# The last layer of a stacked cross network: tail sums by GpSimd, four row tiles in column tiles, another order of row tiles and stores

## The chip, the cores and the metric

The kernel runs on one core of one Trainium2 chip. Its time is the device time of one execution in microseconds (us); the median of several executions is given. A profile is one more execution, recorded by the hardware profiler; its span reaches from the first to the last recorded event of the program, and is shorter than the execution's own time.

The engines are TensorE (PE; the loads of its stationary operand are shown as PEld), VectorE (DVE), ScalarE (ACT), GpSimd (POOL) and SyncE (SP). Matmuls write PSUM, which has eight banks of 128 partitions by 512 float32; GpSimd does not read PSUM in this kernel.

## The reference

Six layers of a cross network over 4096 rows of 416 features (26 fields of 16), all in bfloat16:

```python
B, F, D, L = 4096, 26, 16, 6
Din = min(F * D, 1024)              # 416
x0: (B, Din)   ws: (L, Din, Din)   bs: (L, Din)

def reference(x0, ws, bs):
    x = x0
    for l in range(ws.shape[0]):
        x = x0 * (x @ ws[l] + bs[l]) + x
    return x
```

Since every layer adds a multiple of x0, x after layer l is x0 * (1 + the sum of all x @ w + b so far). The kernel keeps that sum, in PSUM.

## The kernel before

**Tiling.** The rows are worked in four blocks of 1024 (NS, SB), each block through all six layers before the next. The 416 features are three chunks of 128 (`CH`) and a tail of 32. Inside a block the data lies transposed: features on partitions, rows along the free dimension, in two halves of 512 rows. Six PSUM banks hold the running sums of the main chunks, bank 3h + m for half h and chunk m; banks 6 and 7 hold those of the tail, four groups of 256 rows stacked on 32 partitions each. Bank contents stay over the layers: each layer's matmuls add to them.

**One layer.** `main` (288) multiplies one chunk pair in four column tiles: four matmuls, each with 32 columns of weights, write one strip of 32 partitions each, at tile position (0, 32q). `tail_rows` (302) adds the tail features' share, in row tiles: 32 partitions of the contraction at position (32q, 0), with all 128 columns. `tail_outs` (344) makes the tail's own sums, in column tiles. A switch between column tiles, row tiles and the whole array happens several times in a layer. `leave` (404) then makes the next x of a chunk on DVE: (sum + bias) * x0. `leave_tail` (426) does it for the tail: ACT adds the bias in two halves (`tail_halves`, 417; one half for each of banks 6 and 7) and writes the float32 tile `t32`, and GpSimd multiplies it by x0. `cb` holds 1 plus the running sums of the biases, one column for each layer; its chunk NC is the tail's.

**The last layer of the last block.** The first three blocks leave their results transposed and turn them by DMA. The last block's last layer is computed in row form instead, so that no turn is needed: eight tiles of 128 rows by 416 features, one PSUM bank each, `ROW_BANKS` (580): tile 0 has bank 6, tile 1 bank 7, tiles 2 to 7 banks 0 to 5. Each tile is a sum of three parts:

- `row_main` (584): x of layer 5 (128 features by 128 rows, stationary) times the weights (416 wide, moving), three matmuls.
- `row_sums` (594): the running sums up to layer 4, which lie transposed in `sS` as bfloat16, are turned by a product with the identity matrix, three matmuls with 128 moving columns.
- `row_tails` (604): the tail's share of the product and the tail's running sums `st`, four row groups at once, for tiles 0, 2, 4, 6 and then for tiles 1, 3, 5, 7. The matmul that opens a bank carries a start flag.

`keep_sum` (440) makes `sS` from the main banks, plus the last layer's bias, and `tail_halves(L - 1, st_sb, ...)` (565) makes `st` from the tail banks. These run in the branch `ending` (529, 564 to 574): ACT does the two halves of `st`, the three sums of the first half of rows and one of the second; DVE does the other two. A bank can be overwritten by a row tile when its sums are read out.

`finish` (626) multiplies a tile by x0's rows (`xr`): DVE does six tiles straight from PSUM; tiles 1 and 3 are copied by ACT to float32 and multiplied by GpSimd. `store_rows` (645) stores finished tiles, 104 KB each.

**What sets the order.** Each engine runs its instructions in the order in which the program adds them (`Plan.add`, 28); a table of readers and writers puts in the semaphore waits. A reader of a PSUM bank also waits for the earlier readers of that bank. A DMA waits on the queue of the engine that issues it, and what stands behind it on that queue waits too. The order of the last layer is written out by hand at 652 to 673: PE does mains 0 to 3, sums 0 to 3, main 4, the row tails, sums 4, and then main and sums of tiles 5, 6, 7. Tiles 1 and 3 stand on ACT ahead of ACT's stores. The stores are SP: tiles 0 and 1; ACT: 2 and 3; SP: 4 and 5; ACT: 6; SP: 7. At last SP waits for all landings.

Of the kernel before, what the change touches and what calls it, by code (L numbers as in the profile page):

```python
# [6 lines left out]
FP32 = mybir.dt.float32  # L7
ALU = mybir.AluOpType
# [110 lines left out]
def bass_standalone__dcn_v2_cross__recsys_kernel(  # L119
# [7 lines left out]
    L = ws.shape[0]  # L127
    NC = 3
# [13 lines left out]
    with ExitStack() as es:  # L142

        def sb(name, shape, dt=BF16):
            return es.enter_context(nc.sbuf_tensor(name, shape, dt))
# [22 lines left out]
        bsa_sb = sb("bsa_sb", [L + 1, D])  # L168
        u_sb = sb("u_sb", [L + 1, L])
        cb_sb = sb("cb_sb", [128, NC + 1, L], FP32)  # L170
        ps = es.enter_context(nc.psum_tensor("ps", [128, 8, 512], FP32))
        psT = ps.bitcast(BF16)

# [4 lines left out]
        def quad(q):  # L178
            return slice(32 * q, 32 * q + 32)
# [78 lines left out]
        def mm(pe, dst, lhsT, rhs, start, pos=None):  # L258
            return pe.matmul(  # L259
                dst, lhsT=lhsT, rhs=rhs, start=start, stop=True, skip_group_check=True,  # L260
                tile_position=pos,
            )
# [154 lines left out]
        def tail_halves(l, dst, key):  # L417
            for h in HALVES:
                p = slice(64 * h, 64 * h + 64)
                P.add(  # L420
                    "scalar", lambda e, p=p, h=h: e.activation(  # L421
                        out=dst[p, :], in_=ps[p, T_BANK[h], 0:G], func=ACTF.Identity, bias=cb_sb[p, NC, l:l + 1]
                    ), reads=[("ps", T_BANK[h]), ("cb",)], parts=[key],
                )
# [15 lines left out]
        def keep_sum(h, c, eng):  # L440
            o, i, b = sS_sb[:, c, h * H:(h + 1) * H], ps[:, bank(h, c), :], cb_sb[:, c, L - 1:L]
            if eng == "scalar":
                fn = lambda e: e.activation(out=o, in_=i, func=ACTF.Identity, bias=b)
            else:
                fn = lambda e: e.tensor_scalar_add(o, i, b)
            P.add(eng, fn, reads=[("ps", bank(h, c)), ("cb",)], writes=[("sS", c, h)])
# [80 lines left out]
        for s in range(NS):  # L527
            for l in range(L):
                ending = s == NS - 1 and l == L - 2
                if s == NS - 1 and l == L - 1:  # L530
                    break
                if s == 0 and l == 0:
                    for k in CH:
                        for m in CH:
                            main(s, l, 0, m, k)
                        if k == 0:
                            bias_sums()
                        if k == 1:
                            tail_in(0)
                    tail_outs(s, l, True)  # L540
                    tail_rows(s, l, False)
                    for c in CH:
                        leave(s, l, 0, c)
                else:
                    for m in CH:
                        for k in CH:
                            main(s, l, 0, m, k)
                    tail_rows(s, l, l == 0)
                    for c in CH:
                        leave(s, l, 0, c)  # L550
                    tail_outs(s, l, False)
                if l == 2 and s < NS - 1:
                    tail_in(s + 1)
                leave_tail(s, l, not ending)
                if l == 2 and s < NS - 1:
                    keep_tail_in(s + 1)
                if s == 0 and l == 0:
                    corner(2, L, "wt2")
                if l == 1 and s > 0:
                    store_block(s - 1)  # L560
                if s < NS - 1 and l in (3, 4):
                    g = 2 * (l - 3)
                    swap(x0t_sb[:, s + 1], ("x0t", s + 1), tuple("scalar" if q // 2 == l - 3 else None for q in range(4)))
                if ending:
                    tail_halves(L - 1, st_sb, ("st",))
                    for c in CH:
                        keep_sum(0, c, "scalar")
                for m in CH:
                    for k in CH:
                        main(s, l, 1, m, k)  # L570
                    leave(s, l, 1, m)
                if ending:
                    for c in CH:
                        keep_sum(1, c, ("scalar", "vector", "vector")[c])
            if s < NS - 1:
                transpose_block(s)

# [3 lines left out]
        src, off = src_main(s, l)  # L581
        srct, tkey = src_tail(s, l)

        def row_main(j, start):
            b, h = ROW_BANKS[j], j // 4
            for k in CH:
                P.add(
                    "tensor", lambda pe, k=k: mm(
                        pe, ps[:, b, 0:D], src[:, k, off + j * 128:off + (j + 1) * 128], w_sb[:, l, k, :],
                        start and k == 0,  # L590
                    ), reads=[("w", l), src_key(s, l, k, h)], adds=[("ps", b)],
                )

        def row_sums(j):
            b, h = ROW_BANKS[j], j // 4

            def fn(pe):
                for c in CH:
                    ins = mm(pe, ps[:, b, c * 128:(c + 1) * 128], sS_sb[:, c, j * 128:(j + 1) * 128], ident[:, :], False)
                return ins  # L600

            P.add("tensor", fn, reads=[("ident",)] + [("sS", c, h) for c in CH], adds=[("ps", b)])

        def row_tails():
            for r in range(2):
                def fn(pe, r=r):
                    for g in range(4):
                        b = ROW_BANKS[2 * g + r]
                        mm(
                            pe, ps[:, b, 0:D], srct[quad(g), 0, r * 128:(r + 1) * 128], wt_sb[quad(g), l, :],  # L610
                            2 * g + r > 4, (32 * g, 0),
                        )
                    for g in range(4):
                        b = ROW_BANKS[2 * g + r]
                        ins = mm(
                            pe, ps[:, b, DF:D], st_sb[quad(g), r * 128:(r + 1) * 128], ident[quad(g), quad(g)],
                            False, (32 * g, 0),
                        )
                    return ins

                P.add(
                    "tensor", fn, reads=[("wt", wkey(l)), tkey, ("st",), ("ident",)],
                    adds=[("ps", ROW_BANKS[2 * g + r]) for g in range(4)],
                )

        def finish(j, by_pool):
            b, jj = ROW_BANKS[j], (NS - 1) * JS + j
            if by_pool is None:
                P.add(
                    "vector", lambda e: e.tensor_tensor(  # L630
                        out=o_sb[:, jj, :], in0=ps[:, b, 0:D], in1=xr_sb[:, j, :], op=ALU.mult
                    ), reads=[("ps", b), ("xr",)], writes=[("ol", j)],
                )
                return
            t = f32_sb[:, by_pool, :]
            P.add(
                "scalar", lambda e: e.activation(out=t, in_=ps[:, b, 0:D], func=ACTF.Copy),  # L637
                reads=[("ps", b)], writes=[("f32", by_pool)],
            )
            P.add(  # L640
                "gpsimd", lambda e: e.tensor_tensor(out=o_sb[:, jj, :], in0=t, in1=xr_sb[:, j, :], op=ALU.mult),  # L641
                reads=[("f32", by_pool), ("xr",)], writes=[("ol", j)],
            )

        def store_rows(queue, a, b):
            ja = (NS - 1) * JS
            P.add(
                queue, lambda e: e.dma_start(out_v[:, ja + a:ja + b, :], o_sb[:, ja + a:ja + b, :]),
                reads=[("ol", j) for j in range(a, b)], writes=[("outl", a)], dma="outl%d" % a,
            )  # L650

        for j in range(4):
            row_main(j, True)
        for j in range(4):
            row_sums(j)
        row_main(4, True)
        row_tails()
        finish(0, None)
        finish(1, 0)
        finish(2, None)  # L660
        finish(3, 1)
        row_sums(4)
        finish(4, None)
        for j in range(5, 8):
            row_main(j, False)
            row_sums(j)
            finish(j, None)
        store_rows("sync", 0, 2)
        store_rows("scalar", 2, 4)
        store_rows("sync", 4, 6)  # L670
        store_rows("scalar", 6, 7)
        store_rows("sync", 7, 8)
        P.add("sync", None, reads=[("out", s) for s in range(NS - 1)] + [("outl", a) for a in (0, 2, 4, 6, 7)])

        P.emit(nc, es)

# [27 lines left out]
```

## Time and profile before

| | us |
|---|---|
| median of 3 runs | 130.01 (129.94, 130.01, 130.77) |
| the profiled execution, its own time | 130.68 |
| its span | 129.4 |
| PE busy (matmuls) | 124.5, 96% of the span |
| DVE, ACT, POOL busy | 98.9, 50.5, 38.7 |
| first matmul of the row tiles starts | 119.69 |
| row tails start on PE | 123.10 |
| last matmuls of tile 7 start (three) | 125.70 |
| first product of `finish` on DVE | 123.54 |
| last product of `finish` on DVE, start and duration | 126.07, 0.59 |
| stores issued by SP | 125.39, 125.81, 126.69 |
| stores issued by ACT | 126.33, 126.79 |
| from issue to landing, stores of `o_sb` at 648 (least, median, most) | 2.1, 2.4, 2.6 |

Times in the timeline count from the span's start. A line of the timeline has start, duration, engine, line of the kernel, operation, output <- inputs, shapes and how many instructions were merged; for a matmul, 128*32 is a stationary operand of 128 rows by 32 columns (a column tile), 32*128 a row tile, 128*128 the whole array. What stands in brackets is the engine's idle time before the line and who ended it. SPq and ACTq are those engines' queues, where the duration is that of issuing, not of the transfer. TensorE's granted clock was 1.00 throughout.

### The profile page before, as it was taken

The page shows a single profiled execution, that of the slowest core. Times are in us where ns is not written, and L with a number is a line of the kernel's source. Part 1 is how long each engine was busy: PE and PEld are TensorE (multiplying, and loading weights), DVE is VectorE, ACT ScalarE, POOL GpSimd, SP SyncE. Part 2 cuts the span into 40 slices and gives each one's busy share as a digit, 9 for nine tenths or more (in the row PEclk, how much of TensorE's full clock was granted, in tenths as well). Part 3 has the DMA queues.
Part 4 walks back from the last instruction along what each step waited for, and adds up shares of the span by engine and source line. Part 5 has one row for each costly group of instructions (what it writes and reads, how often), then busy time and mean ns, then how long its engine had stood idle before and what let it go on. Part 6 is the DMA issues. An engine that isn't in the chain of part 4 may idle for free.

```text
span 129.4 us, 5183 instructions
## 1 busy us (share of the span) xinstructions
PE 124.5 (96%) x2352; PEld 64.3 (50%) x2352; DVE 98.9 (76%) x151; ACT 50.5 (39%) x113; POOL 38.7 (30%) x86
## 2 busy tenths in 40 slices
PE   6999999999999999999999999999999999999990
PEld 4544545545545545545545545545545545544650
DVE  0309879779779779788788788798797797797881
ACT  1525225455505224464514233463513243245720
POOL 6044344044024053043123152142122152242050
PEclk9999999999999999999999999999999999999999
DMA  3989999999729307000019208000009507000007
GB/s 111 232 206 223 145 245 213 173 195 170 221 51 156 64 11 262 5 0 5 0 39 193 42 0 268 0 5 0 5 16 132 120 5 263 5 0 5 0 0 263
DMA packets 34065, 13.11 MB, mean 101 GB/s; under 512 B 25334, under 2 KB 34044, under 8 KB 34044
## 3 DMA queue, kind: packets, MB, share of 16 engines
q1 hardware_dynamic: 33248, 12.20, 45.2%
q10 hardware_dynamic: 796, 0.59, 1.4%
q8 instruction: 18, 0.29, 1.0%
q14 instruction: 3, 0.02, 0.1%
HBM read 4.07 MB, written 3.41 MB: 58 GB/s over the span
## 4 chain that ended last, share of the span: by engine, by line
PE 92%; DVE 2%; DMA 2%; ACT 0%; issue 0%
PE ps L259 91%; DVE o_sb L630 2%; DMA xin_sb<-in_x_dram 2%; PE ps L482 1%; ACT x0t_sb L382 0%; PE ps L267 0%
## 5 line engine op out<-in xcount | busy, mean ns | idle before, releaser
L411 DVE SCALAR_TENSOR_TENSOR xT_sb<-ps,cb_sb,x0T_sb 128x512 bf16<-128x512 f32 x120 | 80.9, 743 | 19.8 <-PE ps L259 19.8
L259 PE MATMUL ps<-xT_sb,w_sb 128*32 128x512 bf16 (+1 forms) x1596 | 84.6, 364 | 0.0
L259 PEld LDWEIGHTS ps<-xT_sb,w_sb 128*32 128x32 bf16 x1596 | 40.8, 97 | 37.2 <-issue 4.0
L421 ACT ACTIVATE t_sb<-ps,cb_sb 64x256 f32<-64x256 f32 x46 | 21.6, 470 | 51.1 <-PE ps L259 50.9
L434 POOL TENSOR_TENSOR xt_sb<-t_sb,x0t_sb 128x256 bf16<-128x256 f32 x20 | 13.4, 672 | 63.8 <-ACT t_sb L421 63.8
L398 ACT ACTIVATE xt_sb<-xt_sb 32x256 bf16<-32x256 bf16 x38 | 15.7, 414 | 15.4 <-POOL xt_sb L434 15.2
L259 PE MATMUL ps<-x0T_sb,w_sb 128*32 128x512 bf16 (+1 forms) x336 | 19.5, 373 | 0.1
L400 POOL COPY xt_sb<-xt_sb 32x256 bf16<-32x256 bf16 x38 | 15.0, 394 | 2.4
L411 DVE SCALAR_TENSOR_TENSOR xo_sb<-ps,cb_sb,x0T_sb 128x512 bf16<-128x512 f32 x18 | 12.1, 743 | 2.5 <-PE ps L259 2.5
L259 PEld LDWEIGHTS ps<-x0T_sb,w_sb 128*32 128x32 bf16 x336 | 8.4, 97 | 8.1 <-issue 0.8
L259 PE MATMUL ps<-xt_sb,wt_sb 32*128 32x512 bf16 (+1 forms) x152 | 11.6, 326 | 0.0
L259 PE MATMUL ps<-xt_sb,wc_sb 32*128 32x256 bf16 x76 | 7.3, 268 | 0.0
L259 PEld LDWEIGHTS ps<-xt_sb,wt_sb 32*128 32x128 bf16 x152 | 2.3, 91 | 8.1 <-DVE xT_sb L411 6.4
L259 PE MATMUL ps<-w_sb,xT_sb 128*128 128x416 bf16 x24 | 5.0, 339 | 0.0
L434 POOL TENSOR_TENSOR xot_sb<-t_sb,x0t_sb 128x256 bf16<-128x256 f32 x3 | 2.0, 674 | 9.9 <-ACT t_sb L421 9.9
L398 ACT ACTIVATE x0t_sb<-x0t_sb 32x256 bf16<-32x256 bf16 x12 | 4.9, 410 | 0.1
L252 POOL COPY wc_sb<-wt_sb 32x32 bf16<-32x32 bf16 (+1 forms) x12 | 2.8, 234 | 5.5 <-DMA wt_sb<-in_ws_dram 4.9
L267 PE MATMUL ps<-ones_sb 128*128 128x256 bf16 x12 | 2.9, 419 | 1.3 <-DVE ones_sb L228 1.3
L259 PEld LDWEIGHTS ps<-xt_sb,wc_sb 32*128 32x128 bf16 x76 | 3.9, 93 | 0.3
L497 DVE COPY x0T_sb<-ps 128x256 bf16<-128x256 bf16 x4 | 1.2, 292 | 3.6 <-PE ps L482 3.4
L630 DVE TENSOR_TENSOR o_sb<-ps,xr_sb 128x416 bf16<-128x416 f32 x6 | 3.1, 584 | 1.0 <-PE ps L259 1.0
L641 POOL TENSOR_TENSOR o_sb<-f_sb,xr_sb 128x416 bf16<-128x416 f32 x2 | 1.9, 976 | 4.8 <-ACT f_sb L637 4.8
(40 smaller groups left out, 34.5 us busy)
## 6 DMA issues: line engine op xcount, KB each, us to landing
out_dram<-o_sb SPq DMA_DIRECT2D x3, 832.0 KB, 4.2
w_sb<-in_ws_dram SPq DMA_DIRECT2D x6, 312.0 KB, 5.0
xr_sb<-in_x_dram SPq DMA_DIRECT2D x1, 832.0 KB, 5.8
wt_sb<-in_ws_dram SPq DMA_DIRECT2D x4, 104.0 KB, 3.1
out_dram<-o_sb SPq DMA_DIRECT2D x2, 208.0 KB, 2.2
xin_sb<-in_x_dram ACTq DMA_DIRECT2D x1, 208.0 KB, 3.2
xin_sb<-in_x_dram SPq DMA_DIRECT2D x1, 208.0 KB, 2.9
out_dram<-o_sb ACTq DMA_DIRECT2D x1, 208.0 KB, 2.4
```

Of the source, the lines that this page charges most:

```text
L252: "gpsimd", lambda e, p=p, g=g: e.tensor_copy(out=wc_sb[p, a:b, g % 2, quad(g)], in_=wt_sb[p, a:b, DF:D]), reads=[("wt", name), ("wc", nam ...
L259: return pe.matmul(dst, lhsT=lhsT, rhs=rhs, start=start, stop=True, skip_group_check=True, tile_position=pos,)
L267: ins = pe.matmul(ps[:, 7, 0:256], lhsT=ones_sb[:, 0:128], rhs=ones_sb[:, :], start=True, stop=True)
L398: fn = lambda e, d=dst, s=src: e.activation(out=d, in_=s, func=ACTF.Copy)
L400: fn = lambda e, d=dst, s=src: e.tensor_copy(out=d, in_=s)
L411: "vector", lambda e: e.scalar_tensor_tensor(out=dst, in0=ps[:, bank(h, c), :], scalar=cb_sb[:, c, l:l + 1], in1=x0T_sb[:, c, o:o + H], op ...
L421: "scalar", lambda e, p=p, h=h: e.activation(out=dst[p, :], in_=ps[p, T_BANK[h], 0:G], func=ACTF.Identity, bias=cb_sb[p, NC, l:l + 1]), re ...
L434: "gpsimd", lambda e: e.tensor_tensor(out=dst, in0=t, in1=x0t_sb[:, s, 0, :], op=ALU.mult),
L482: ins = pe.transpose(out=psT[:, b, j * 128:(j + 1) * 128], in_=xin_sb[:, 2 * i + j, c * 128:(c + 1) * 128], identity=ident[:, :],)
L497: "vector", lambda e, d=dst, s=src: e.tensor_copy(out=d, in_=s),
L630: "vector", lambda e: e.tensor_tensor(out=o_sb[:, jj, :], in0=ps[:, b, 0:D], in1=xr_sb[:, j, :], op=ALU.mult), reads=[("ps", b), ("xr",)], ...
L641: "gpsimd", lambda e: e.tensor_tensor(out=o_sb[:, jj, :], in0=t, in1=xr_sb[:, j, :], op=ALU.mult),
```

## The change

In the branch `ending`, `st` is no longer made by ACT from PSUM. GpSimd makes it from `t32`, which holds the same sums plus layer 4's bias: it subtracts two columns of `cb` into a new tile `bt` of 128x1, and adds that to `t32`. Sum (1, 1) goes from DVE to ACT. The mains and sums of row tiles 0 to 3 are each cut into four column tiles of 32 rows; tiles 4 to 7 stay whole. The mains of tile 4 come behind the row tails instead of ahead of them, so that each of the tiles 4 to 7 has its sums right behind its mains; tile 4's bank is opened by the row tails. The stores are six instead of five, in another order and on other queues.

```diff
--- before.py
+++ after.py
@@ -168,6 +168,7 @@
         bsa_sb = sb("bsa_sb", [L + 1, D])
         u_sb = sb("u_sb", [L + 1, L])
         cb_sb = sb("cb_sb", [128, NC + 1, L], FP32)
+        bt_sb = sb("bt_sb", [128, 1], FP32)
         ps = es.enter_context(nc.psum_tensor("ps", [128, 8, 512], FP32))
         psT = ps.bitcast(BF16)
 
@@ -562,7 +563,15 @@
                     g = 2 * (l - 3)
                     swap(x0t_sb[:, s + 1], ("x0t", s + 1), tuple("scalar" if q // 2 == l - 3 else None for q in range(4)))
                 if ending:
-                    tail_halves(L - 1, st_sb, ("st",))
+                    P.add(
+                        "gpsimd", lambda e: e.tensor_tensor(
+                            out=bt_sb[:, :], in0=cb_sb[:, NC, L - 1:L], in1=cb_sb[:, NC, L - 2:L - 1], op=ALU.subtract
+                        ), reads=[("cb",)], writes=[("bt",)],
+                    )
+                    P.add(
+                        "gpsimd", lambda e, t=t32_sb[:, l % 2, :]: e.tensor_scalar_add(st_sb[:, :], t, bt_sb[:, :]),
+                        reads=[("t32", l % 2), ("bt",)], writes=[("st",)],
+                    )
                     for c in CH:
                         keep_sum(0, c, "scalar")
                 for m in CH:
@@ -571,7 +580,7 @@
                     leave(s, l, 1, m)
                 if ending:
                     for c in CH:
-                        keep_sum(1, c, ("scalar", "vector", "vector")[c])
+                        keep_sum(1, c, ("scalar", "scalar", "vector")[c])
             if s < NS - 1:
                 transpose_block(s)
 
@@ -581,22 +590,31 @@
         src, off = src_main(s, l)
         srct, tkey = src_tail(s, l)
 
-        def row_main(j, start):
+        def row_mm(pe, dst, lhsT, rhs, start, narrow):
+            if not narrow:
+                return mm(pe, dst, lhsT, rhs, start)
+            for q in range(4):
+                ins = mm(pe, dst[quad(q)], lhsT[:, quad(q)], rhs, start, (0, 32 * q))
+            return ins
+
+        def row_main(j, start, narrow):
             b, h = ROW_BANKS[j], j // 4
             for k in CH:
                 P.add(
-                    "tensor", lambda pe, k=k: mm(
+                    "tensor", lambda pe, k=k: row_mm(
                         pe, ps[:, b, 0:D], src[:, k, off + j * 128:off + (j + 1) * 128], w_sb[:, l, k, :],
-                        start and k == 0,
+                        start and k == 0, narrow,
                     ), reads=[("w", l), src_key(s, l, k, h)], adds=[("ps", b)],
                 )
 
-        def row_sums(j):
+        def row_sums(j, narrow):
             b, h = ROW_BANKS[j], j // 4
 
             def fn(pe):
                 for c in CH:
-                    ins = mm(pe, ps[:, b, c * 128:(c + 1) * 128], sS_sb[:, c, j * 128:(j + 1) * 128], ident[:, :], False)
+                    ins = row_mm(
+                        pe, ps[:, b, c * 128:(c + 1) * 128], sS_sb[:, c, j * 128:(j + 1) * 128], ident[:, :], False, narrow
+                    )
                 return ins
 
             P.add("tensor", fn, reads=[("ident",)] + [("sS", c, h) for c in CH], adds=[("ps", b)])
@@ -608,7 +626,7 @@
                         b = ROW_BANKS[2 * g + r]
                         mm(
                             pe, ps[:, b, 0:D], srct[quad(g), 0, r * 128:(r + 1) * 128], wt_sb[quad(g), l, :],
-                            2 * g + r > 4, (32 * g, 0),
+                            g >= 2, (32 * g, 0),
                         )
                     for g in range(4):
                         b = ROW_BANKS[2 * g + r]
@@ -650,27 +668,22 @@
             )
 
         for j in range(4):
-            row_main(j, True)
+            row_main(j, True, True)
         for j in range(4):
-            row_sums(j)
-        row_main(4, True)
+            row_sums(j, True)
         row_tails()
         finish(0, None)
         finish(1, 0)
         finish(2, None)
         finish(3, 1)
-        row_sums(4)
-        finish(4, None)
-        for j in range(5, 8):
-            row_main(j, False)
-            row_sums(j)
+        for j in range(4, 8):
+            row_main(j, False, False)
+            row_sums(j, False)
             finish(j, None)
-        store_rows("sync", 0, 2)
-        store_rows("scalar", 2, 4)
-        store_rows("sync", 4, 6)
-        store_rows("scalar", 6, 7)
-        store_rows("sync", 7, 8)
-        P.add("sync", None, reads=[("out", s) for s in range(NS - 1)] + [("outl", a) for a in (0, 2, 4, 6, 7)])
+        STORES = (("scalar", 2, 3), ("sync", 0, 2), ("sync", 4, 6), ("sync", 3, 4), ("scalar", 6, 7), ("sync", 7, 8))
+        for queue, a, b in STORES:
+            store_rows(queue, a, b)
+        P.add("sync", None, reads=[("out", s) for s in range(NS - 1)] + [("outl", a) for _, a, _ in STORES])
 
         P.emit(nc, es)
```

## The prediction

> **What bounds the kernel now.** I read the page first, then the chain of work that ended last, then the timeline of the last 12 us engine by engine, then the DMA share in narrow windows behind the last matmul.
>
> ```profile
> span 129.4 us, 5183 instructions
> ...
> PE 92%; DVE 2%; DMA 2%; ACT 0%; issue 0%
> ```
>
> TensorE carries the span almost to its end. The change touches only the last layer of the last block, so only what follows 118.8 us can move; the rest of the chain is the same program. There the timeline of PE reads (start, duration, matmuls; the matmul ends are modelled, so I use starts):
>
> ```profile
> 119.37 0.39 PE L259 MATMUL ps<-xT_sb,w_sb 128*32 128x512 bf16 x4
> 119.69 0.35 PE L259 MATMUL ps<-w_sb,xT_sb 128*128 128x416 bf16 x1
> ```
> ```profile
> 121.81 0.83 PE L259 MATMUL ps<-ident,sS_sb 128*128 128x128 bf16 x12
> ...
> 122.48 0.69 PE L259 MATMUL ps<-w_sb,xT_sb 128*128 128x416 bf16 x3
> ...
> 123.10 0.35 PE L259 MATMUL ps<-wt_sb,xt_sb 32*128 32x416 bf16 x4
> ...
> 123.61 0.34 PE L259 MATMUL ps<-ident,sS_sb 128*128 128x128 bf16 x3
> ...
> 125.18 0.69 PE L259 MATMUL ps<-w_sb,xT_sb 128*128 128x416 bf16 x3
> ```
>
> PE hardly waits for an operand here (the loads idle 0.2 once for ACT, at 121.73, and no matmul starts later for it). The reader is to see the paces: 12 full main matmuls from 119.69 to 121.81 (0.177 each), 12 sums to 122.48 (0.056 each), and from 123.61 on one tile per 0.695 (main parts of tiles 5, 6, 7 start at 123.79, 124.48, 125.18). A group of four 512-wide column matmuls goes every 0.215 us: 14 of them from 113.63 to 116.75 take 3.12, less one 0.10 for the switch at the end. So the first full matmul should have come at 119.37 + 0.215 = 119.585; it came at 119.69. That 0.10 is the price of a change from column tiles to another tiling. Behind PE:
>
> ```profile
> 118.85 0.96 ACT L421 ACTIVATE st_sb<-ps,cb_sb 64x256 bf16<-64x256 f32 x2
> ...
> 119.83 2.42 ACT L443 ACTIVATE sS_sb<-ps,cb_sb 128x512 bf16<-128x512 f32 x4
> ...
> 121.18 1.40 DVE L445 TENSOR_SCALAR sS_sb<-ps,cb_sb 128x512 bf16<-128x512 f32 x2
> ...
> 123.54 3.12 DVE L630 TENSOR_TENSOR o_sb<-ps,xr_sb 128x416 bf16<-128x416 f32 x6 [0.96 <-PE ps L259]
> ...
> 124.34 1.91 POOL L641 TENSOR_TENSOR o_sb<-f_sb,xr_sb 128x416 bf16<-128x416 f32 x2 [4.77 <-ACT f_sb L637]
> ...
> 125.39 1.65 SPq L648 DMA_DIRECT2D out_dram<-o_sb  x3
> ...
> 126.33 0.97 ACTq L648 DMA_DIRECT2D out_dram<-o_sb  x2
> ```
>
> The first store leaves only at 125.39, behind GpSimd's first product (124.34 + 0.98). ACT's second store, of tile 6, leaves at 126.79 behind ACT's first, which waited for GpSimd's second product (end 126.25). And then the DMA engines (last but one column their share):
>
> ```profile
> 126.20:126.30 0.10, 0.00 (x0) 0.00 (x0) 0.10 (x1) 0.00 (x0) 0.05 (x1) 1.00 0.15 50
> 126.30:126.70 0.40, 0.00 (x0) 0.00 (x0) 0.36 (x1) 0.00 (x0) 0.00 (x0) 1.00 0.99 316
> ...
> 128.30:128.70 0.40, 0.00 (x0) 0.00 (x0) 0.00 (x0) 0.00 (x0) 0.00 (x0) 1.00 0.94 340
> ...
> 128.80:128.90 0.10, 0.00 (x0) 0.00 (x0) 0.00 (x0) 0.00 (x0) 0.00 (x0) 1.00 0.16 42
> ```
>
> This is the reading that decides. From 126.28 to 128.85 all 16 DMA engines are full: eight tiles of 104 KB at 0.32 us each. The end is not the last product at 126.66 plus the latency of one store. It is the first store's issue (125.39), 0.89 until its first packet, 2.57 of full DMA, and 0.5 until the last landing at 129.37 (126.79 plus the 2.6 that the DMA view gives the ACT store of 104 KB). Earlier first stores are worth more than an earlier last product.
>
> **The change, part by part.**
>
> *Tail sums on GpSimd.* Two ACT operations go (0.98 from 118.85 to 119.83, gaps included). GpSimd gets a 128x1 subtraction and a 128x256 addition behind its product that ends at 118.90 + 0.67 = 119.57. No row shows either. Lower bound: its 32x32 copy (0.21) and its 128x256 copy (0.40); upper: twice its 128x416 product (0.98). I take 0.21 + 0.67 (the product of the same 128x256 shape from f32) and 0.1 of hand-overs: st is ready at 120.5, between 120.2 and 121.5. It is needed at 122.48 (below), so slack of 1.0 hides it; past that, PE would stand for the excess.
>
> *Hidden-part sums.* ACT starts its sums at 118.85 instead of 119.83 and does five at 0.58 spacing: the last ends 118.85 + 4 x 0.58 + 0.69 = 121.86. The new wait is that sum (1,1) follows DVE's work on the same bank, over at 120.60, before ACT comes to it at 121.17. DVE's single sum still starts at 121.18, ending 121.92. Before, the last sum ended at 122.58. Row tails write all these banks, so without this edit they would have to wait at 122.48.
>
> *Column tiles for tiles 0 to 3.* 24 matmuls become 96 in 24 groups of four. The trace has the very shape of the new sums, 128 rows by 32 columns with 128 moving, at the head of the kernel:
>
> ```profile
> 7.89 0.22 PE L259 MATMUL ps<-ident,xin_sb 128*32 128x128 bf16 x2
> ...
> 7.94 0.22 PE L259 MATMUL ps<-ident,xin_sb 128*32 128x128 bf16 x2
> ...
> 8.11 0.39 PE L259 MATMUL ps<-x0T_sb,w_sb 128*32 128x512 bf16 x4
> ```
>
> Four groups go from 7.89 to 8.11: 0.055 each, against 0.056 for a full sum. The 416-wide group is not in the trace; between 0.055 at 128 and 0.215 at 512 the straight line gives 0.175, against 0.177. So the groups cost nothing, and the switch at 119.69 goes: mains start at 119.585. The switch now comes at the row tails, where full to row tiles already cost 0.09 (122.83 + 0.177 to 123.10). Net: 0.10 off the PE stream. Bounds: +0.65 if a 128-wide group paced like the 256-wide ones (0.109, twelve times 0.054), -0.12 at best.
>
> A rule of the Trainium skill speaks against this part: TensorEngine Tiling (Array Packing), Restrictions and Gotchas, says that column tiling excludes the fast weight load, and TensorE: Matmul & The Clock Gate, LDWEIGHTS, puts the nanoseconds of a load at its number of columns divided by 1.2. By it four 32-column loads in series would be an estimated 107 ns per sum group, some 0.6 us over twelve, and the time 129.6. The trace's 97 ns for a 32-column load beside 98 for a full one, overlapped at 0.055 per group, decides for no cost.
>
> *Row tails before tile 4.* Tile 4's mains (0.53) move behind the row tails; their sums were there already, and tile 4's bank is now opened by the tails. PE: 119.585 + 12 x 0.177 = 121.71; + 12 x 0.056 = 122.38; + 0.10 switch: row tails at 122.48, 0.62 earlier. PE's end moves 0.10 only: 122.48 + 0.51 (123.10 to 123.61) = 122.99, and tile 7's mains start 3 x 0.695 later at 125.08 against 125.18. But the first four products move by 0.62: DVE starts at 122.92, GpSimd's products end at 124.70 and 125.63. DVE, which ran back to back, now follows PE: tile 5 done at 125.15, tile 6 at 125.85, tile 7 at 125.97 + 0.59 = 126.56.
>
> *Stores.* ACT: tile 2 at about 124.05 (DVE's second product, 123.42 + 0.58, +0.05), then tile 6 at 125.88, no longer behind GpSimd. SP: tiles 0,1 at 124.76 (GpSimd's first), 4,5 at 125.20, tile 3 at 125.70 (GpSimd's second), tile 7 at 126.59. One more issue costs SP up to 0.46; it ends at 126.16, and what stands behind it is tile 7's, so GpSimd may be 0.4 late before this wait counts. One more landing is waited for, all long before the last. Packets, 0.89 behind each issue and 0.32 a tile: tile 2 over at 125.3, tiles 0,1 at 126.3, 4,5 at 126.9, 3 at 127.25, 6 at 127.57, 7 at 127.89; plus 0.5, landed at 128.39. The engines stand idle for a while at first; the backlog before tile 7 is 0.1.
>
> The Trainium skill (DMA: Bandwidth & Descriptors, Anatomy of one DMA) has 2.0 us plus bytes over 436 GB/s, fitted on another issuing path; an estimate from it for 104 KB is 2.24, and the time would be 129.5. The first store here, 208 KB with nothing ahead of it, landed in 2.1, so the rows make 1.74 of a free tile.
>
> **Sum.** The span ends at 128.41 instead of 129.39: -1.0. The profiled execution took 130.68 (1.29 around its span), 0.67 above the median of 130.01; I carry the difference over: 129.7 for a profiled one, 129.0 at the median.
>
> **Rivals.**
> - *The last store keeps its flight.* If a store takes 2.4 to 2.6 whatever is queued, only its issue counts: 126.59 + 2.4 = 129.0, or 0.2 earlier than ACT's 126.79 with 2.6. Time 129.6 to 129.8. For it: the last three stores all took that long. Against: full engines explain it, and the first took 2.1.
> - *Small groups go slower* than at the head, where only four came in a row and here twelve do: up to +0.65 on PE, 129.1 to 129.7.
> - *Slower: the strips' loads do not overlap in a long run.* A group then costs four loads, 4 x 0.097 = 0.39. At the sums alone +4.0, at the mains +2.5 more: 133.0 to 135.5. It decides from 0.08 a sum group on (12 x 0.08 takes the 1.0). Against: 0.055 in the head, and twenty layers of column groups at 0.215.
> - *The tail sums come late.* GpSimd's addition with a scalar from memory would have to take 2.6 instead of 0.67 before PE stands; at four times the product's time, 130 to 131.
>
> **How the numbers follow.** The sum 0.68 (own range 128.6 to 129.4: a tile landing in 1.65 to 1.9, and 0.3 of spread); last store's flight 0.15; slower small groups 0.09; loads 0.05; late tail sums 0.03. Range: the bound of the sum, -1.1, with 0.3 of spread gives 128.6; the flight rival's end gives 129.8; outside are the last two and the edges. A measurement of this kernel tells about 1% (1.3 us) from no change. Faster by that needs 128.7, a quarter of the first case: 0.17. Slower is the loads and a little of the tail sums: 0.06. The same: 0.77.
>
> **What would show it.** First row main at 119.58 in 128*32 tiles; sum groups 0.055 apart; row tails near 122.5; DVE from 122.9 with gaps between its products; first store near 124.05 on ACT; DMA share below full before 126.3 and little backlog behind 127.5; tile 7 landing 1.8 after its issue. I am wrong if that store still takes 2.4, if sum groups are over 0.06 apart, if row tails wait for GpSimd, or if tile 7's store stands behind tile 3's.

## The result, and the profile after

The changed kernel takes 129.56 us (median of 22 runs, 128.95 to 130.62) against 130.24 us (22 runs, 129.92 to 131.42). The medians differ by 0.68 us. The ratio of the runs is 0.9939 with a 95% interval of 0.9916 to 0.9962, which makes some 0.8 us: inside 1%, as forecast, and 0.2 short of the forecast 1.0. The profiled execution took 130.38 us, its span 129.1.

The spans of the two profiles differ by only 0.3 us, and that is no contradiction. The profile after lost 0.55 in the first layers, in work that the change does not touch (last section). So I count from a point that both share, the start of the last group of 512-wide column matmuls of layer 5 on PE, and call it **A**: 119.37 before, 119.92 after. The span ends at A + 10.02 before and at A + 9.22 after: 0.80, which agrees with the timing. The timeline of PE after, from A on:

```profile
119.92 0.39 PE L260 MATMUL ps<-xT_sb,w_sb 128*32 128x512 bf16 x4
120.13 0.35 PE L260 MATMUL ps<-w_sb,xT_sb 128*32 128x416 bf16 x4
```
```profile
122.24 0.84 PE L260 MATMUL ps<-ident,sS_sb 128*32 128x128 bf16 x48
123.02 0.35 PE L260 MATMUL ps<-wt_sb,xt_sb 32*128 32x416 bf16 x4
...
123.53 0.35 PE L260 MATMUL ps<-w_sb,xT_sb 128*128 128x416 bf16 x1
```

The first main now comes 0.21 behind A, not 0.32: no switch. Twelve main groups take 2.11, twelve groups of sums and the later switch 0.78, and the row tails start at A + 3.10 (A + 3.73 before). The other engines:

```profile
119.41 3.00 ACT L444 ACTIVATE sS_sb<-ps,cb_sb 128x512 bf16<-128x512 f32 x5
...
124.58 2.23 ACTq L666 DMA_DIRECT2D out_dram<-o_sb  x2
```
```profile
120.09 0.19 POOL L567 TENSOR_TENSOR bt_sb<-cb_sb 128x1 f32<-128x1 f32 x1
120.38 0.93 POOL L572 TENSOR_SCALAR st_sb<-t_sb,bt_sb 128x256 bf16<-128x256 f32 x1
124.26 1.90 POOL L659 TENSOR_TENSOR o_sb<-f_sb,xr_sb 128x416 bf16<-128x416 f32 x2 [2.95 <-ACT f_sb L655]
```
```profile
123.46 3.65 DVE L648 TENSOR_TENSOR o_sb<-ps,xr_sb 128x416 bf16<-128x416 f32 x6 [0.99 <-PE ps L260]
```
```profile
125.30 2.18 SPq L666 DMA_DIRECT2D out_dram<-o_sb  x4
```

The six products took 3.12 back to back before; now they take 3.65, because they start 0.63 earlier and then follow PE. The first store leaves at A + 4.66 instead of A + 6.02. Tile 7's leaves at 127.14, A + 7.22, against A + 7.42 for the last one before. Now the DMA engines, in the same windows table (share in the last column but one), and then tile 7's store alone:

```profile
125.40:125.80 0.40, 0.40 (x7) 0.27 (x5) 0.32 (x1) 0.00 (x0) 0.40 (x1) 1.00 0.72 252
125.80:126.10 0.30, 0.30 (x3) 0.19 (x2) 0.28 (x1) 0.00 (x0) 0.30 (x1) 1.00 0.07 20
...
126.90:127.30 0.40, 0.00 (x0) 0.00 (x0) 0.21 (x1) 0.00 (x0) 0.00 (x0) 1.00 1.06 349
...
128.10:128.50 0.40, 0.00 (x0) 0.00 (x0) 0.00 (x0) 0.00 (x0) 0.00 (x0) 1.00 0.76 244
```
```profile
L666 SPq DMA_DIRECT2D out_dram<-o_sb x1: 350/350/350, 127.1 to 127.1; - x1
...
DMA to landing us min/median/max: 1.8/1.8/1.8
```

Tile 2 is through at 125.9, the engines pause, the other seven tiles follow, and little backlog is left when tile 7's packets come: its store lands 1.85 after its issue. Tile 2's store, with nothing ahead of it, took 1.74; the last three stores before took 2.4 to 2.6.

### The profile page after: what moved, and what is told of

It is laid out like the page before. It is cut to its first block, busy times and chain, and to the rows that moved or that the text cites. A ratio compares the mean times of both kernels' runs of the same rounds, so it can differ in the third digit from the quotient of the medians.

```text
span 129.1 us, 5328 instructions
## 1 busy us (share of the span) xinstructions
PE 124.2 (96%) x2424; PEld 64.5 (50%) x2424; DVE 98.5 (76%) x150; ACT 50.0 (39%) x112; POOL 39.6 (31%) x88
## 4 chain that ended last, share of the span: by engine, by line
PE 88%; SPq 5%; DMA 4%; issue 0%; DVE 0%
PE ps L260 88%; DMA w_sb<-in_ws_dram 4%; SPq L187 3%; SPq L205 2%; DVE o_sb L648 0%
## 5 line engine op out<-in xcount | busy, mean ns | idle before, releaser
L260 PE MATMUL ps<-w_sb,xT_sb 128*32 128x416 bf16 (+1 forms) x60 | 5.1, 339 | 0.0
L444 ACT ACTIVATE sS_sb<-ps,cb_sb 128x512 bf16<-128x512 f32 x5 | 3.0, 689 | 0.0
```

What stands on the lines that cost most here:

```text
L260: return pe.matmul(dst, lhsT=lhsT, rhs=rhs, start=start, stop=True, skip_group_check=True, tile_position=pos,)
```

## The experiments

PE's work is the same in all kernels up to A, so the columns behind A count from it. Each ratio is to runs of the kernel before taken beside that kernel (their medians lie between 130.24 and 130.68); the intervals of most of the kernels overlap, so it is the columns from A that tell them apart.

| kernel | A | row tails | first store | tile 7's store | its time to landing | end | ratio, 95% interval |
|---|---|---|---|---|---|---|---|
| before | 119.37 | 3.73 | 6.02 | 7.32 | 2.38 | 10.02 | 1 |
| changed | 119.92 | 3.10 | 4.66 | 7.22 | 1.85 | 9.22 | 0.9939 (0.9916 to 0.9962) |
| before, new stores | 118.67 | 3.73 | 5.29 | 7.50 | 2.20 | 9.85 | 0.9979 (0.9962 to 0.9997) |
| changed, old stores | 119.42 | 3.10 | 5.39 | 7.22 | 2.16 | 9.54 | 0.9961 (0.9942 to 0.9979) |
| changed, whole tiles | 119.37 | 3.21 | 4.77 | 7.32 | 1.86 | 9.33 | 0.9935 (0.9906 to 0.9963) |
| changed, main 4 first | 119.19 | 3.63 | 5.19 | 7.40 | 2.20 | 9.74 | 0.998 (0.9964 to 0.9997) |
| changed, tail sums by ACT | 118.84 | 3.15 | 4.71 | 7.26 | 1.85 | 9.27 | 0.9925 (0.9886 to 0.9964) |
| changed, late stores | 119.44 | 3.10 | 5.83 | 7.30 | 2.53 | 9.98 | 0.9977 (0.9955 to 0.9998) |
| changed, four additions | 119.91 | 4.59 | 6.15 | 8.71 | 1.85 | 10.72 | one run, 131.97 us |
| changed, sorted waits | 118.92 | 3.10 | 4.66 | 7.22 | 1.85 | 9.11 | 0.9899 (0.9864 to 0.9933) |

There is one profile of each kernel. Two of them were profiled a second time (last experiment), and there the columns from A came again within 0.01.

The ends with new stores, old stores, main 4 first and late stores came 0.03 to 0.05 past the ranges expected for them: all four ranges leave out the 0.15 between the last landing and the end of the span (last experiment).

**The six stores alone.** The kernel before with

```diff
-        store_rows("sync", 0, 2)
-        store_rows("scalar", 2, 4)
-        store_rows("sync", 4, 6)
-        store_rows("scalar", 6, 7)
-        store_rows("sync", 7, 8)
+        STORES = (("scalar", 2, 3), ("sync", 0, 2), ("sync", 4, 6), ("sync", 3, 4), ("scalar", 6, 7), ("sync", 7, 8))
+        for queue, a, b in STORES:
+            store_rows(queue, a, b)
```

> The kernel before with the six reordered stores alone. Times count from the last 512-wide column group of layer 5 on PE, called A (119.37 before, 119.92 after); the span ends at A + 10.02 before and A + 9.22 after. Theory (the stream of stores sets the end: 0.89 from issue to first packet, 0.32 a tile while the DMA engines are full, 0.5 to the landing): only tile 2's store gets off early (about A + 5.35); the other seven tiles still start behind GpSimd's first product, at A + 6.9, and take 7 x 0.32, so the end comes at A + 9.7 to 9.8, some 0.3 sooner than before. Rival 1 (only the last store's issue and a fixed flight of 2.4 count): tile 7's issue comes at A + 7.45 behind tile 3's on SP, end at A + 9.85 to 9.9. Rival 2 (the order on PE is all that counts): no change, A + 10.0.

The last landing came at A + 9.70, the end at A + 9.85: 0.17 sooner than before. The end alone lies in the first rival's range (A + 9.85 to 9.9) and 0.05 past the stream's; the landing tells them apart: with the rival's flight of 2.4 it would have come at A + 9.90. Tile 7's store leaves later than any store of the kernel before (A + 7.50, behind tile 3's on SP) and still lands 0.30 sooner than the last one did: by the stream, because one tile is out of the way. Six tiles still stand on SP behind GpSimd's first product, and tile 6's store, on ACT, leaves at A + 6.79.

**The old stores in the changed kernel.** The same edit backwards.

> The changed kernel with the five old stores. Theory (stream): the first store leaves at A + 5.39, its packets start at A + 6.28, eight tiles at 0.32 make A + 8.85, plus 0.5: the end at A + 9.35 to 9.5, so 0.15 to 0.3 of the 0.8 is given back, and the DMA share is full without a pause from A + 6.3 to A + 8.85. Rival (the reordered stores are the whole gain): the end goes back to A + 9.9 to 10.0. Rival (the order on PE and the products are the whole gain): A + 9.22, no change.

End at A + 9.54: 0.32 of the 0.80 is given back, neither nothing nor all. The windows of this kernel show the stream without a pause from its first packet to its last:

```profile
125.70:126.10 0.40, 0.28 (x4) 0.10 (x2) 0.30 (x2) 0.00 (x0) 0.00 (x0) 1.00 0.97 310
126.10:126.90 0.80, 0.00 (x0) 0.00 (x0) 0.51 (x1) 0.00 (x0) 0.00 (x0) 1.00 1.06 344
126.90:127.70 0.80, 0.00 (x0) 0.00 (x0) 0.00 (x0) 0.00 (x0) 0.00 (x0) 1.00 1.04 350
127.70:128.20 0.50, 0.00 (x0) 0.00 (x0) 0.00 (x0) 0.00 (x0) 0.00 (x0) 1.00 0.94 332
128.20:128.40 0.20, 0.00 (x0) 0.00 (x0) 0.00 (x0) 0.00 (x0) 0.00 (x0) 1.00 0.12 33
```

From 125.70 to 128.30 there are eight tiles in 2.6 us, as before the change, only 0.6 earlier: the first store leaves at A + 5.39 instead of A + 6.02.

**Tiles 0 to 3 on the whole array.**

```diff
-            row_main(j, True, True)
+            row_main(j, True, False)
-            row_sums(j, True)
+            row_sums(j, False)
```

> The changed kernel with row tiles 0 to 3 on the whole array again. Theory: the paces are the same (0.176 a main, 0.056 a sum), only the switch from column tiles comes 0.10 to 0.11 earlier and a second one stays at the row tails, so everything behind moves by 0.10: row tails at A + 3.20 instead of 3.10, the end at A + 9.32. Rival (the column tiles themselves are slower or faster at a tile): the interval from first main to the row tails differs by more than 0.03 from 2.89.

End at A + 9.33, 0.11 later. The first main comes 0.32 behind A again, and from there to the row tails it is 2.88 against 2.89 in column tiles. The lines of this kernel (A is 119.37) beside those above: the same paces, moved by the switch.

```profile
121.81 0.83 PE L260 MATMUL ps<-ident,sS_sb 128*128 128x128 bf16 x12
122.57 0.35 PE L260 MATMUL ps<-wt_sb,xt_sb 32*128 32x416 bf16 x4
```

So 48 small matmuls in a row keep the pace of 12 whole ones, and the switch is all that the column tiles are worth. The ratio does not separate this kernel from the changed one; the trace does.

**Tile 4's mains ahead of the row tails.** In column tiles, with the start flag where it was (`2 * g + r > 4`):

```diff
+        row_main(4, True, True)
         row_tails()
...
-            row_main(j, False, False)
+            if j > 4:
+                row_main(j, False, False)
```

> The changed kernel with tile 4's mains ahead of the row tails again (in column tiles, so that no switch is added). Theory: PE's last sums stay within 0.05 of A + 6.34, but the first four products come 0.53 later, so the first stores do too; tiles 0 and 1 leave at A + 5.9, seven tiles follow each other from A + 6.8 on, tile 3's store delays tile 7's by 0.1 to 0.15, and the end comes at A + 9.55 to 9.7. Rival (only the last product and a free flight count): the end moves by no more than tile 7's issue, 0 to 0.15, A + 9.22 to 9.37.

End at A + 9.74: 0.52 of the 0.80, the largest loss among the four steps that were undone one by one. PE's last sums start at A + 6.34 in both kernels, and DVE's last product at A + 6.60 in both. DVE's line is the one of the kernel before, back to back (A is 119.19):

```profile
123.26 3.12 DVE L648 TENSOR_TENSOR o_sb<-ps,xr_sb 128x416 bf16<-128x416 f32 x6 [1.52 <-PE ps L260]
```

The end of PE's and DVE's work did not move; what moved is the first store, from A + 4.66 to A + 5.19, and GpSimd's products by 0.53. Tile 7's store then leaves 0.18 later behind tile 3's, and takes 2.20 instead of 1.85. That is the 0.52.

**Tail sums by ACT, sum (1, 1) by DVE.**

```diff
+                    tail_halves(L - 1, st_sb, ("st",))
...
-                        keep_sum(1, c, ("scalar", "scalar", "vector")[c])
+                        keep_sum(1, c, ("scalar", "vector", "vector")[c])
```

(GpSimd's two instructions are taken out.)

> The changed kernel with the tail sums by ACT from PSUM and sum (1, 1) on DVE, as before. Times count from A, the last 512-wide column group of layer 5 on PE; the changed kernel ends at A + 9.22, its row tails start at A + 3.10. Theory: mains wait for nothing, tile 1's bank being read out at A + 0.44; ACT's third sum ends at A + 2.3, just as sums 0 start, and DVE's second at A + 3.21, so the row tails start at A + 3.25 to 3.3 instead of 3.10 and the end moves by the same 0.15 to 0.2, to A + 9.37 to 9.45. Rival (ACT and DVE had room, the edit is worth nothing): A + 9.22.

End at A + 9.27, only 0.05 later: a miss. The row tails do not wait for DVE's second sum (over at A + 3.21), because only the second half of them writes its bank. The 0.05 is the wait of sums 0 for ACT's third sum: they start at A + 2.36 instead of A + 2.32, as this kernel's weight loads show:

```profile
121.19 0.68 PEld L260 LDWEIGHTS ps<-ident,sS_sb 128*32 128x32 bf16 x48 [0.28 <-ACT sS_sb L444]
```

**The same six stores, held back.** The rival of a fixed flight says that only tile 7's issue counts; the stream says that the first issue does.

```diff
-        STORES = (("scalar", 2, 3), ("sync", 0, 2), ("sync", 4, 6), ("sync", 3, 4), ("scalar", 6, 7), ("sync", 7, 8))
+        STORES = (("sync", 4, 6), ("sync", 0, 2), ("scalar", 6, 7), ("scalar", 2, 3), ("sync", 3, 4), ("sync", 7, 8))
```

> The changed kernel with the same six stores, but none leaves before tiles 4 and 5 are done: SP has 4 and 5, 0 and 1, 3, 7, and ACT has 6, 2. Tile 7's issue stays within 0.1 of A + 7.22. Theory (stream): first issue at A + 5.83, packets from A + 6.72, eight tiles at 0.32 to A + 9.29, plus 0.5: the end at A + 9.8 to 9.95, 0.6 to 0.7 later, with a full DMA share from A + 6.7 on, and tile 7's store takes 2.4 or more from issue to landing instead of 1.85. Rival (each store has a flight of its own and they overlap): the end stays within 0.1 of A + 9.22.

End at A + 9.98: 0.76 later, with tile 7's issue moved by 0.08. The first issue at A + 5.83 fills the engines from 126.2 until 128.7, and tile 7's store takes 2.5:

```profile
126.20:126.60 0.40, 0.00 (x0) 0.00 (x0) 0.40 (x1) 0.00 (x0) 0.00 (x0) 1.00 1.00 318
...
128.20:128.60 0.40, 0.00 (x0) 0.00 (x0) 0.00 (x0) 0.00 (x0) 0.00 (x0) 1.00 0.95 340
```
```profile
DMA to landing us min/median/max: 2.5/2.5/2.5
```

The order of PE, the tiling and the tail sums are those of the changed kernel here, and nearly the whole gain is gone. The rival falls.

**GpSimd's addition four times.** The second instruction is added in a loop of four.

> The changed kernel with GpSimd's addition of the tail sums made four times over (the same values into the same tile). Theory: the addition takes 0.93, so st is ready at A + 1.39 + 3 x 0.93 to 0.96 = A + 4.2 to 4.3; the row tails wait for it and start about 0.06 later, at A + 4.3, 1.2 later than the A + 3.10 of the changed kernel, and the end moves by 1.1 to 1.2. One addition had 1.7 of room. Rival (PE does other work meanwhile, or the tail sums are not what the row tails wait for): less than 0.3.

The row tails start at A + 4.59 and the end comes at A + 10.72, 1.50 later: the way is right, the size 0.3 too small. Each addition waits for the one before, since they write the same tile, and they follow each other at 1.02 instead of 0.93 to 0.96, and the row tails start 0.14 behind the last instead of 0.06. PE's line names the wait:

```profile
124.50 0.36 PE L260 MATMUL ps<-wt_sb,xt_sb 32*128 32x416 bf16 x4 [1.43 <-POOL st_sb L573]
```

So one addition, over at A + 1.39, had 1.7 us of cover before A + 3.10.

**SP's last waits, sorted.**

```diff
-        P.add("sync", None, reads=[("out", s) for s in range(NS - 1)] + [("outl", a) for _, a, _ in STORES])
+        P.add("sync", None, reads=[("out", s) for s in range(NS - 1)] + [("outl", a) for _, a, _ in STORES]).waits.sort(
+            key=lambda w: (w.dma.startswith("outl"), [a for _, a, _ in STORES].index(int(w.dma[4:])) if w.dma.startswith("outl") else 0)
+        )
```

> The changed kernel with SP's last waits sorted: the three blocks' stores first, then the last stores in the order of their landing, tile 7 at the end. In the changed kernel tile 7 landed 0.15 before the span's end, because SP had waited for it ahead of three waits that were long over. Theory: the span ends 0.02 to 0.04 behind tile 7's landing, at A + 9.10, 0.12 sooner (0.1% of the time, within the interval of the timing). Rival (the end is set by something other than SP's waits): A + 9.22.

Tile 7 lands at A + 9.07 in both kernels; the end comes at A + 9.11 instead of A + 9.22. The 0.9899 of the table is more than 0.11 us can make, so both kernels were run once more, side by side.

> The changed kernel once more, on one chip with the sorted waits of the next run. It ends at A + 9.22. Theory: everything up to A is the same program in all kernels, and the place of A wanders by over 1 us between profiles, so the ratio to the kernel before falls anywhere from 0.990 to 0.996 with the chip and the hour; the one of the next run lies 0.001 below this one, within both intervals.

> The sorted waits once more, beside the changed kernel. Theory: A + 9.11, a ratio 0.001 below that of the changed kernel in the same call. Rival (the 0.990 measured for it against 0.994 for the changed kernel is its own gain): 0.004 below, intervals apart.

They ended at A + 9.22 and A + 9.12, with ratios 0.9958 (0.9933 to 0.9982) and 0.9945 (0.9922 to 0.9968). The difference of 0.004 between the two ratios did not come again: it is 0.001 here, with overlapping intervals, as expected. By the traces the sorted waits end 0.1 us sooner than the changed kernel; the timing alone cannot show it.

## Why the prediction was right, point by point

**The mechanism** held: before, the end was set by the stream of stores, counted from the first issue. Late stores (0.76 lost with only the order of the stores changed) and main 4 first (0.52 lost with PE's end unchanged) show it. In the changed kernel the pause at 125.9 cuts the stream in two, and it is tiles 0 and 1 that start the second part: their issue at A + 5.38, 0.89 to the first packet, seven tiles at 0.32 and 0.5 to the landing make A + 9.01, and tile 7 landed at A + 9.07. Tile 7's own issue (A + 7.22) with the 1.74 of a store that has nothing ahead of it makes A + 8.96, so there the last product and the stream count almost alike; by these numbers a faster stream alone could win an estimated 0.1. The rival of the fixed flight falls by the changed kernel itself, 1.85.

**The sum** was 0.98 and the trace has 0.80. The issues came within 0.02 of the forecast, counted from A: tile 2 at 4.66 (4.68), tiles 0 and 1 at 5.38 (5.39), 4 and 5 at 5.83 (5.83), 3 at 6.32 (6.33), 6 at 6.53 (6.51), 7 at 7.22 (7.22). Tile 7 landed at A + 9.07 (9.02). The other 0.13 is a term that the sum mis-sized: it let the span end 0.02 behind the last landing, as before, and it ended 0.15 behind. "One more landing is waited for, all long before the last" looked at when the stores land and not at the order in which SP waits for them. Before, SP's very last wait was for tile 6's store, the last to land. After, two more of SP's waits (three were expected), for four landings that were over, stand behind the one for tile 7, and each ends 0.06 behind the one before it. The sorted waits give back 0.11.

**Column tiles.** Paces of 0.176 and 0.056 and a switch of 0.10 were read from rows, and whole tiles gave 2.88 against 2.89 for the paces and 0.11 at the end for the switch. So both rivals on the loads and on small groups fall. The Trainium skill's rule (TensorEngine Tiling (Array Packing), Restrictions and Gotchas) that column tiling excludes the fast weight load may hold; no run here shows whether it does. The 0.6 us that the prediction estimated for loads in series does not appear: in the changed kernel the 48 loads of the sums take 0.097 each and are all over within 0.84, so they overlap.

**Row tails before tile 4** was forecast as 0.10 at PE's end and 0.62 at the products; PE's last sums came 0.10 earlier, DVE's first product 0.63. That the step is worth most was not said so plainly: undone, it costs 0.52. Undone one by one, the steps cost 0.52, 0.32, 0.11 and 0.05, 1.00 together for 0.80: the order and the stores empty the same queue, so they cannot be added.

**Tail sums.** The addition took 0.93, not 0.67, and st was ready at A + 1.39 instead of A + 1.13, inside the bounds; with 1.7 of cover it cost nothing. The step that failed is the one on the sums: "without this edit they would have to wait at 122.48". They would not, since the first half of the row tails does not touch the bank of the late sum. The two edits together are worth 0.05 (0.15 to 0.2 was expected of undoing them), and by ACT's third sum.

**The time.** 129.0 was forecast from a median of 130.01; over 22 runs that median is 130.24, which makes 0.2 of the 0.56 between 129.0 and 129.56. The gain makes the rest: 0.68 between the medians where 1.0 was forecast.

## What to carry to other kernels

When the last stores land one after the other at an even spacing and the DMA share is full between them, the end is the issue of the first store behind the last pause plus all the bytes that follow; a queue head that waits for the slowest engine can cost more than a late last product. Order the work so that finished pieces leave early, even where the compute's own end does not move, and count the order of the last waits too. When the gain is below the spread of the runs, measure from a point in the trace behind which alone the kernels differ.

## What the runs showed of the hardware that was not expected

The place of A wanders from 118.67 to 119.92 over these profiles, though PE runs the same program up to it; the changed kernel alone had 119.92 and 118.77. From the first matmul of the second layer to A it is 107.43 to 107.45 in all twelve profiles, so the wandering lies ahead of that. Of the kernels above, the two with the latest A (119.92 and 119.91) had PE wait for the second layer's weights; the changed kernel's line, and the same stretch of the kernel before with new stores (A at 118.67):

```profile
12.47 1.90 PE L260 MATMUL ps<-xT_sb,w_sb 128*32 128x512 bf16 x30 [0.66 <-DMA w_sb<-in_ws_dram]
```
```profile
11.24 2.12 PE L259 MATMUL ps<-xT_sb,w_sb 128*32 128x512 bf16 x36
```

The weights landed at 12.4 in these two and between 10.4 and 11.2 in the other ten. That one landing, and not the change, is why the two spans look only 0.3 apart. It is not the whole of the wandering: in the other ten profiles A still lies between 118.67 and 119.44. What differs there is PE's pace at the start. The first three 512-wide column groups begin 0.40 and 0.43 apart before (the first at 5.63), and 0.23 and 0.21 apart with new stores (the first at 5.46). The trace's first record of a granted clock, of 1.00, begins at 7.12 in the one and at 4.73 in the other (the windows view prints 1.00 ahead of it too). Over the ten profiles this record begins between 4.73 and 7.41, and the later it begins, the later, on the whole, the second layer starts, from 11.24 to 12.00. Why the landing and the record come late in some executions was not tried. Also, GpSimd takes longer to add one value per partition to a 128x256 float32 tile (0.93) than to multiply two such tiles, one of them bfloat16 (0.67).
